# A recurrent attention and a cosine feed-forward on one core: eight chunks' bonus sums by TensorE, a fifth buffer for r, k and decays, first units in halves, a new plan of a block

## The chip, the cores and the metric

The kernel runs on one core of a Trainium2 chip. The metric is the device time of one execution in microseconds, the median of several runs; lower is better. Engines are named as in the profile: PE is TensorE (its weight loads apart as PEld), DVE is VectorE, ACT is ScalarE, POOL is GpSimd, SP is SyncE, which here only issues DMAs (SPq).

## The reference, cut to what matters

Two stages. The first is a linear recurrence with a decay per channel and a bonus `u` for the current step; the second is a feed-forward layer with `h * cos(h)` between two products.

```python
# r, k, v, w: (4 batches, 8 heads, 768 steps, 48)
for t in range(S):
    kt, vt, rt, wt = k[:, :, t], v[:, :, t], r[:, :, t], w[:, :, t]
    cur = einsum('bhd,bhe->bhde', u[None] * kt, vt)
    y[:, :, t] = einsum('bhd,bhde->bhe', rt, state + cur)
    state = wt[:, :, :, None] * state + einsum('bhd,bhe->bhde', kt, vt)
x = y as (3072 tokens, 384)
h = x @ w_in                 # (3072, 2048)
out = (h * cos(h)) @ w_out   # (3072, 384)
```

## The kernel before

**Chunks and blocks.** Time is cut into chunks of 128 steps; a chunk is one batch's 128 steps with all eight heads, as four pairs of heads. There are 24 chunks, in an order in which chunks 0 to 3 are the first of the four batches, 4 to 7 the second, and so on. Two chunks make a block (`BLK = 2`), so there are 12 blocks of 256 tokens: block 0 holds chunks 0 and 1, block 3 chunks 6 and 7.

**A chunk's steps**, by the letters that the plan uses:

- `load`: one DMA brings r, k and the decays, transposed, into a tile of the tag `tt` (`BUFS` gives four of them; 112 x 1541 numbers). `lv` loads v, `lr` loads r and k once more in natural layout (`rk`, in a buffer of the tag `h`, which the weights' words use too).
- `decay`: on DVE a scan backwards (`ee`, L208), its least value kept (L212), a reciprocal (L213), a scan forwards (L214); then r is multiplied by the forward products (`r3`, L218, DVE in the start and POOL later) and k by the backward ones (`k3`, L219).
- `diag`: the bonus sum r * u * k over a head's 48 channels, one number per step and head (`cd`). For chunks below `BY_PE` it is a product on DVE (`rkt`, L205) and a small matmul with u (`pc`, L225), copied out by ACT. For the others it is two products and a reduction on DVE from `rk` (L230, L231, L233). POOL then spreads `cd` over the diagonal of `asb` (L237).
- `a`: the scores, r against k (`pa`, L260), whose part above the diagonal DVE copies into `asb` (L262).
- `o` and `p`: what the chunk's own steps give (`py`, L315 and L320) and what the state gives (L330, L334), then the result as a high part (`xT`, ACT) and a low part (DVE, L144).
- `t` and `s`: k transposed (`pt`, L269, copied out as `kn`), then the chunk's addition to the state (`pst`, L287), and the new state `sn` (L292, L294). `d` (`dd`, L250) multiplies the state by the whole decay of the next chunk, on DVE in the start and on POOL later; ACT copies it to where `p` reads it.

**Units.** The 2048 columns between the products are 16 slices of 128; a block passes them two at a time, in 8 units. `mm1` is 18 matmuls into a bank of the kind `h` (`ph`, L382), 9 for each slice; then the gate: ACT (L358), DVE (L359), ACT (L360), DVE (L361), ACT (high part `gs`, L141), POOL (low part `gs`, L144, two instructions). `mm2` is 12 matmuls into two accumulators (`acc`, L400), of which the last four read the low part. Every product is three passes over high and low parts.

**Weights.** The 16 slices arrive as 64 bit numbers (`raw`) and are taken apart once, in the start (`w`): three instructions on ACT (L163, L166, L167) and a copy (L141), and three on DVE (L168, L169, and the low part L144) each. In the start the program's letters `f` and `w` fetch and take apart one slice.

**Order.** PE's order is written by hand throughout; DVE, ACT, POOL and SP are put in order by a scheduler, from the order in which the program is written and its own costs. `START` writes the first 16 units, which belong to blocks 0 and 1 in turns (`PAIR`), with chunks 0 to 7 between them. From block 2 on, `PLAN` has one row for each of a block's 8 units: `mm1`, an `mm2` that runs three units behind, and steps of chunks counted from the block's own, so `decay+4` in block 2 is that of chunk 8. A step that has not been done is done when another needs it (`NEEDS`).

**Banks.** In the start five banks serve attention; when block 0's first `mm2` comes it is three, while blocks 0 and 1 are both open two of each kind, and after block 1's last `mm2` three of each.

## Time and profile before

| | |
|---|---|
| time, median of 3 runs | 572.29 us (571.83 to 575.41) |
| the profiled execution's own time | 573.05 us |
| its span, first to last instruction | 571.2 us |
| mean granted TensorE clock over the span | 0.97 |
| PE busy, matmuls | 524.2 us, 92% of the span |
| DVE busy | 378.7 us, 66% |
| ACT busy | 270.1 us, 47% |
| POOL busy | 233.2 us, 41% |

The span is 1.85 us shorter than the time of the same execution. A busy PE is not a PE at its peak, and a share over the whole span hides stages of different kinds: up to about 66 us the weights are taken apart, up to about 145 us blocks 0 and 1 run side by side, and from there ten blocks run one after the other.

### The profile page before, as it was taken

Reading aid. Unit: us, or ns where it says so; the run is one execution under the profiler, and the core shown is the slowest. Engines: PE = TensorE matmul, PEld = TensorE weight load, DVE = VectorE, ACT = ScalarE, POOL = GpSimd, SP = SyncE. Lnnn points to the kernel's source line nnn. Section 1 sums busy time; section 2 is a strip of 40 time slices with the busy share of each in tenths; the row PEclk is TensorE's granted clock in tenths of the full one; section 3 lists DMA queues with packets and bytes.
Section 4 is the critical chain, followed back from the end, with each engine's and each line's share of the span. In section 5 each row is a group of like instructions: output and inputs, shape, how many; then the busy total and the mean of one; then the engine's idle time right before and its main releaser. Section 6 shows DMA issues by size and latency. Waiting matters only on the chain. (4 is left out here: it accounts for less than half of the span.)

```text
span 571.2 us, 11903 instructions
## 1 busy us (share of the span) xinstructions
PE 524.2 (92%) x4964; PEld 494.8 (87%) x4964; DVE 378.7 (66%) x560; ACT 270.1 (47%) x454; POOL 233.2 (41%) x286
## 2 busy tenths in 40 slices
PE   4658899985999999999999999999999999999996
PEld 3557889975899899899899899999899899999996
DVE  7989899985858558558548649548548447642331
ACT  2877997542342442452453353353352454444542
POOL 3033334463535434534534634534634532324332
PEclk9957899997999999999999999999999999999999
DMA  8955742116033034025025025025024017100000
GB/s 275 343 192 180 210 147 71 55 36 175 33 116 100 0 99 116 2 77 136 1 69 147 0 63 153 1 64 150 1 64 124 0 50 254 63 26 1 29 1 31
DMA packets 16728, 52.17 MB, mean 91 GB/s; under 512 B 2016, under 2 KB 8416, under 8 KB 16672
## 3 DMA queue, kind: packets, MB, share of 16 engines
q1 hardware_dynamic: 16528, 51.28, 29.6%
q8 instruction: 40, 0.66, 0.5%
q14 instruction: 16, 0.13, 0.1%
q10 hardware_dynamic: 144, 0.10, 0.1%
HBM read 46.65 MB, written 4.72 MB: 90 GB/s over the span
## 5 line engine op out<-in xcount | busy, mean ns | idle before, releaser
L144 POOL TENSOR_TENSOR gs<-rr,gs 128x256 fp32r<-128x256 f32 x192 | 157.9, 844 | 205.1 <-ACT gs L141 184.6
L382 PE MATMUL ph<-xT,w 128*128 128x256 f32 x1728 | 226.7, 286 | 15.4 <-ACT w L141 7.0
L382 PEld LDWEIGHTS ph<-xT,w 128*128 128x128 f32 x1728 | 216.7, 191 | 20.5 <-ACT w L141 7.5
L400 PE MATMUL acc<-w,gs 128*128 128x384 f32 x1152 | 226.1, 344 | 6.1 <-POOL gs L144 5.8
L400 PEld LDWEIGHTS acc<-w,gs 128*128 128x128 f32 x1152 | 199.0, 190 | 14.7 <-POOL gs L144 10.3
L360 ACT ACTIVATE rr<-rr,quarter 128x512 f32<-128x512 f32 x96 | 69.4, 723 | 159.7 <-DVE rr L359 159.7
L359 DVE SCALAR_TENSOR_TENSOR rr<-rr,ph 128x512 f32<-128x512 int32 x96 | 65.3, 680 | 70.6 <-ACT rr L358 58.8
L361 DVE TENSOR_TENSOR rr<-rr,ph 128x512 f32<-128x512 f32 x96 | 65.5, 682 | 44.6 <-ACT rr L360 44.3
L358 ACT ACTIVATE rr<-ph 128x512 int32<-128x512 f32 x96 | 57.0, 594 | 63.5 <-PE ph L382 63.4
L141 ACT CAST gs<-rr 128x512 fp32r<-128x512 f32 x96 | 58.8, 613 | 46.3 <-PE acc L400 43.3
L237 POOL TENSOR_SCALAR_AFFINE_SELECT asb<-cd 128x512 f32<-128x512 f32 x48 | 31.2, 674 | 53.2 <-PE py L320 28.0
L208 DVE TENSOR_TENSOR_SCAN ee<-tt,one_e 112x516 f32<-112x516 f32 x24 | 32.7, 1362 | 13.3 <-DMA tt<-tr 13.3
L218 POOL TENSOR_TENSOR tt<-tt 112x512 f32<-112x512 f32 x18 | 29.4, 1632 | 23.5 <-DVE tt L214 20.5
L262 DVE COPY_PREDICATED asb<-mask,pa 128x512 f32<-128x512 uint8 x48 | 32.7, 735 | 5.5 <-PE pa L260 4.2
L214 DVE TENSOR_TENSOR_SCAN tt<-tt,inj 112x516 f32<-112x516 f32 x24 | 34.8, 1452 | 0.1
L260 PE MATMUL pa<-tt 48*128 48x128 f32 x384 | 30.6, 304 | 3.2 <-DVE tt L219 2.2
L250 POOL TENSOR_TENSOR dd<-sn,ee 112x192 f32<-112x192 f32 x18 | 13.5, 753 | 48.9 <-DVE ee L208 48.9
L260 PEld LDWEIGHTS pa<-tt 48*128 48x128 f32 x384 | 25.7, 204 | 8.2 <-issue 4.3
L230 DVE TENSOR_TENSOR rk<-rk 128x384 f32<-128x384 f32 x18 | 15.7, 874 | 20.5 <-DMA rk<-tn 20.5
L287 PEld LDWEIGHTS pst<-v,kn 128*64 128x64 f32 (+1 forms) x320 | 11.4, 141 | 9.1 <-ACT kn L141 7.7
L287 PE MATMUL pst<-v,kn 128*64 128x48 f32 (+1 forms) x320 | 12.9, 233 | 6.9 <-ACT kn L141 6.9
L231 DVE TENSOR_TENSOR rk<-rk,u_sb 128x384 f32<-128x384 f32 x18 | 18.3, 1015 | 0.3
(67 smaller groups left out, 358.4 us busy)
## 6 DMA issues: line engine op xcount, KB each, us to landing
tt<-tr SPq DMA_DIRECT2D x22, 674.2 KB, 7.0
raw<-wts SPq DMA_DIRECT2D x16, 768.0 KB, 7.4
rk<-tn SPq DMA_DIRECT2D x18, 384.0 KB, 3.1
v<-tv SPq DMA_DIRECT2D x24, 224.0 KB, 6.7
ww<-w SPq DMA_DIRECT2D x6, 768.0 KB, 5.1
out<-ob SPq DMA_DIRECT2D x23, 192.0 KB, 2.0
tt<-tr SPq DMA_DIRECT2D x4, 224.0 KB, 4.5
tt<-tr SPq DMA_DIRECT2D x2, 226.2 KB, 3.7
```

What stands on the lines that cost most here:

```text
L141: (nc.scalar.copy if E[name] is nc.scalar else E[name].tensor_copy)(out=out, in_=in_)
L144: E[name].tensor_tensor(out=out, in0=full, in1=high.bitcast(F32), op=ALU.subtract)
L208: nc.vector.tensor_tensor_scan(out=ee.rearrange("p a t -> p (a t)")[:, ::-1], data0=wp[:, 1:W129 + 1][:, ::-1], data1=one_e.rearrange("p a ...
L214: nc.vector.tensor_tensor_scan(out=wp[:, 0:W129], data0=wp[:, 0:W129], data1=inj.rearrange("p a t -> p (a t)"), initial=0.0, op0=ALU.mult, ...
L260: nc.tensor.matmul(out=pa[h][:, p], lhsT=a["k3"][rows(h), p], rhs=a["r3"][rows(h), p], start=True, stop=True)
L262: nc.vector.copy_predicated(a["asb", h], mask, pa[h])
L358: nc.scalar.activation(nn, ph, AF.Copy, scale=INV2PI / W_SCALE, bias=0.25)
L359: nc.vector.scalar_tensor_tensor(out=rr, in0=nn, scalar=-2.0 * math.pi * W_SCALE, in1=ph, op0=ALU.mult, op1=ALU.add)
L360: nc.scalar.activation(rr, rr, AF.Sin, scale=1.0 / W_SCALE, bias=quarter)
L361: nc.vector.tensor_tensor(out=rr, in0=rr, in1=ph, op=ALU.mult)
L382: nc.tensor.matmul(out=ph[:, fi], lhsT=wgt[u * FU + fi][:, 0, a, kt * 128:(kt + 1) * 128], rhs=xT[:, b, kt], start=n == 0, stop=n == 3 * K ...
L400: nc.tensor.matmul(out=accs[i][j][:, :DM], lhsT=gs[:, a, fi, j * C:(j + 1) * C], rhs=wgt[u * FU + fi][:, 1, b], start=u == 0 and fi == 0 a ...
```

## The change

`BY_PE` goes from 6 to 8: chunks 6 and 7 get their bonus sums from `rkt` and `pc`, and no `rk` is loaded for them. `tt` gets a fifth buffer, `cd` and `rkt` a second one; `dd` has two instead of four. From block 2 on `dd` is made by DVE instead of POOL. `mm1` can be called for one slice of a unit; `START` calls it so (`m0`, `m1`), with the bonus sums and scores of chunks 2 and 3 between the halves of the first two units, and the own parts, transposes and state additions of chunks 0 to 3 earlier. `PLAN` has other places for `load`, `d` and `decay`.

```diff
-BY_PE = 6
+BY_PE = 8
...
-BUFS = dict(tt=4, v=4, h=2, rd=2, rr=7, gs=2, asb=4, sn=4, xT=2, kn=4, ee=2, dd=4, cd=1, rkt=1)
+BUFS = dict(tt=5, v=4, h=2, rd=2, rr=7, gs=2, asb=4, sn=4, xT=2, kn=4, ee=2, dd=2, cd=2, rkt=2)
...
-LATER = dict(... dd="p", ...)
+LATER = dict(... dd="v", ...)
...
-PLAN = ["t+2 t+3 mm1 mm2",
+PLAN = ["t+2 t+3 load+6 mm1 mm2",
...
-        "mm1 o+1 mm2 diag+5 p+1 lv+6 load+7 lr+7 load+6 x+2",
...
+        "mm1 o+1 mm2 diag+5 p+1 lv+6 lr+7 x+2",
+        "mm1 s+1 mm2 load+7 lv+7 x+3",
+        "mm1 mm2 d+4",
+        "mm1 mm2 decay+5",
+        "mm1 d+5 mm2 lr+6"]
-START = ["load0 load1 f lv0 decay0 f diag0 a0 lv1 decay1 diag1 a1 w load2 f w o0 mm1",
+START = ["load0 load1 f lv0 decay0 f diag0 a0 lv1 decay1 diag1 a1 w load2 f w o0 x0 decay2 diag2 m0 m1",
...
-    def mm1(t):
+    def mm1(t, part=None):
         i, u = seq[t]
-        weights("f", (u + 1) * FU + LEAD + FLEAD)
...
+        if not part:
+            weights("f", (u + 1) * FU + LEAD + FLEAD)
+            weights("w", (u + 1) * FU + LEAD)
+            for j in range(BLK):
+                att(i * BLK + j, "x")
+            units[t] = bank("h", [C, FU, BT], "ph")
+        xT, ph = xts[i], units[t]
+        for fi in range(FU) if part is None else (part,):
...
-        units[t] = gate(sb, ph)
+        if part is None or part == FU - 1:
+            units[t] = gate(sb, ph)
...
+                elif e in ("m0", "m1"):
+                    mm1(up1[0], int(e[1]))
+                    up1[0] += int(e[1])
```

What this does to the order is seen on the engines. First PE, after the own parts of chunks 0 and 1 (`py`), where the first units of block 0 begin; `w_181`, `w_195` are slices 0 and 1. Before:

```order
L382 MATMUL ph<-xT,w_181 128x256 x9
L382 MATMUL ph<-xT,w_195 128x256 x9
L382 MATMUL ph<-xT,w_278 128x256 x9
L382 MATMUL ph<-xT,w_297 128x256 x9
L225 MATMUL pc<-u_by_head,rkt 128x2 x4
L260 MATMUL pa<-tt 128x128 x8
```

After, up to the first `acc`:

```order
L225 MATMUL pc<-u_by_head,rkt 128x2 x4
L383 MATMUL ph<-xT,w_181 128x256 x9
L383 MATMUL ph<-xT,w_195 128x256 x9
L225 MATMUL pc<-u_by_head,rkt 128x2 x4
L383 MATMUL ph<-xT,w_298 128x256 x9
L260 MATMUL pa<-tt 128x128 x8
L383 MATMUL ph<-xT,w_330 128x256 x9
L260 MATMUL pa<-tt 128x128 x8
```

The bonus sums of chunks 2 and 3 moved ahead of and between the first units, and each chunk's scores stand behind one half of the second unit; before, chunk 3's `pc` and `pa` came only after the first `acc`.

Next DVE, in the last stretch in which blocks 0 and 1 run together, up to the low part of block 2's result (`xT`). Before:

```order
L230 TENSOR_TENSOR rk<-rk 128x384
L231 TENSOR_TENSOR rk<-rk,u_sb 128x384
L361 TENSOR_TENSOR rr<-rr,ph 128x512
L233 TENSOR_REDUCE cd<-rk 128x8 x2
L230 TENSOR_TENSOR rk<-rk 128x384
L231 TENSOR_TENSOR rk<-rk,u_sb 128x384
L230 TENSOR_TENSOR rk<-rk 128x384
L231 TENSOR_TENSOR rk<-rk,u_sb 128x384
L144 TENSOR_TENSOR xT<-py,xT 128x384 x2
```

After:

```order
L231 TENSOR_TENSOR rk<-rk,u_sb 128x384
L230 TENSOR_TENSOR rk<-rk 128x384
L231 TENSOR_TENSOR rk<-rk,u_sb 128x384
L359 SCALAR_TENSOR_TENSOR rr<-rr,ph 128x512
L262 COPY_PREDICATED asb<-mask,pa 128x512 x2
L361 TENSOR_TENSOR rr<-rr,ph 128x512
L359 SCALAR_TENSOR_TENSOR rr<-rr,ph 128x512
L361 TENSOR_TENSOR rr<-rr,ph 128x512
L359 SCALAR_TENSOR_TENSOR rr<-rr,ph 128x512
L361 TENSOR_TENSOR rr<-rr,ph 128x512
L144 TENSOR_TENSOR xT<-py,xT 128x384 x2
```

Of five `rk` products before `xT` two are left, and they stand ahead of four gates' instructions instead of directly before `xT`.

Last DVE in a block from block 2 on, from the low part of the next block's result. Before:

```order
L144 TENSOR_TENSOR xT<-py,xT 128x384 x2
L294 TENSOR_TENSOR sn<-pst,dd 112x192 x2
L233 TENSOR_REDUCE cd<-rk 128x8
L208 SCALAR_TENSOR_TENSOR ee<-tt,one_e 112x516
L359 SCALAR_TENSOR_TENSOR rr<-rr,ph 128x512
```

After:

```order
L144 TENSOR_TENSOR xT<-py,xT 128x384 x2
L294 TENSOR_TENSOR sn<-pst,dd 112x192 x2
L250 TENSOR_TENSOR dd<-sn,ee 112x192 x2
L208 SCALAR_TENSOR_TENSOR ee<-tt,one_e 112x516
L230 TENSOR_TENSOR rk<-rk 128x384
L212 TENSOR_SCALAR wholes<-ee 112x4
```

Two `dd` came in and one reduction went out ahead of the first scan; and a unit's L359 now stands behind `rk` and the scan's small steps.

## Rows read from the trace of the kernel before

**Rows 1.** Busy time in four stretches of the span: the stretch, its length, then PE, PEld, DVE, ACT and POOL busy us with their instructions, the granted clock (a share of 2.4 GHz), the DMA engines' share and GB/s.

```profile
0.00:66.00 66.00, 41.37 (x353) 36.82 (x354) 55.24 (x86) 46.77 (x63) 17.08 (x24) 0.82 0.70 238
66.00:107.00 41.00, 39.12 (x319) 37.97 (x318) 40.69 (x56) 35.19 (x55) 19.16 (x17) 0.99 0.41 121
107.00:145.00 38.00, 29.37 (x302) 27.27 (x301) 29.52 (x44) 11.05 (x22) 15.77 (x21) 0.87 0.34 92
145.00:572.00 427.00, 414.38 (x3996) 392.80 (x3995) 253.24 (x377) 177.10 (x315) 181.21 (x225) 1.00 0.23 66
```

**Rows 2.** The same view for one stretch in which the clock was low.

```profile
134.80:145.10 10.30, 6.73 (x57) 6.22 (x55) 5.92 (x11) 3.19 (x6) 1.93 (x3) 0.50 0.70 181
```

**Rows 3.** PE's waits: line, releaser, us in total, times, the longest.

```profile
PE acc L400 <- POOL gs L144: 5.8, 12, 0.7
```

**Rows 4.** DVE in order of time in the start: start, us, instruction, and in brackets the idle time before it and who ended it.

```profile
41.08 0.69 DVE L205 TENSOR_TENSOR rkt<-tt 112x512 f32<-112x512 f32 x1 [2.58 <-PE pc L225]
49.81 1.33 DVE L262 COPY_PREDICATED asb<-mask,pa 128x512 f32<-128x512 uint8 x2 [1.22 <-POOL asb L237]
64.51 0.62 DVE L292 COPY sn<-pst 112x192 f32<-112x192 f32 x2 [1.44 <-PE pst L287]
105.94 0.93 DVE L144 TENSOR_TENSOR w<-h,w 128x768 fp32r<-128x768 f32 x1
```

**Rows 5.** DVE in order of time from there to block 2's result, as above.

```profile
114.70 2.15 DVE L230 TENSOR_TENSOR rk<-rk 128x384 f32<-128x384 f32 x1
...
121.89 0.67 DVE L361 TENSOR_TENSOR rr<-rr,ph 128x512 f32<-128x512 f32 x1
...
133.26 1.01 DVE L144 TENSOR_TENSOR xT<-py,xT 128x384 fp32r<-128x384 f32 x2
```

**Rows 6.** ACT: the high part of block 2's result, and the copies of the transposed k of chunks 4 and 5.

```profile
126.19 0.86 ACT L141 CAST xT<-py 128x384 fp32r<-128x384 f32 x2
...
138.11 0.85 ACT L141 COPY kn<-pt 128x384 f32<-128x384 f32 x2
```

**Rows 7.** PE in order of time: the bonus sum of chunk 4, and then from the seventh unit of block 1 to the scores of chunk 7.

```profile
88.10 0.95 PE L225 MATMUL pc<-u_by_head,rkt 112*128 112x2 f32 x8
...
113.03 2.37 PE L382 MATMUL ph<-xT,w 128*128 128x256 f32 x18 [0.56 <-DVE rr L361]
...
118.25 2.39 PE L400 MATMUL acc<-w,gs 128*128 128x384 f32 x12
122.71 2.36 PE L382 MATMUL ph<-xT,w 128*128 128x256 f32 x18 [2.07 <-DVE rr L361]
124.91 2.28 PE L400 MATMUL acc<-w,gs 128*128 128x384 f32 x12
127.03 2.29 PE L382 MATMUL ph<-xT,w 128*128 128x256 f32 x18
129.15 2.28 PE L400 MATMUL acc<-w,gs 128*128 128x384 f32 x12
133.87 1.20 PE L269 MATMUL pt<-ident,tt 112*128 112x112 f32 x8 [2.43 <-DVE xT L144]
138.63 1.94 PE L287 MATMUL pst<-v,kn 128*64 128x48 f32 x32 [3.57 <-ACT kn L141]
140.50 1.83 PE L269 MATMUL pt<-ident,tt 112*128 112x112 f32 x8
...
156.50 1.16 PE L260 MATMUL pa<-tt 48*128 48x128 f32 x16 [1.03 <-ACT ob L413]
```

**Rows 8.** DVE behind that: the new states of chunks 4 and 5, and the second unit of block 2.

```profile
140.63 0.62 DVE L294 TENSOR_TENSOR sn<-pst,dd 112x192 f32<-112x192 f32 x2 [2.21 <-PE pst L287]
...
154.65 0.66 DVE L359 SCALAR_TENSOR_TENSOR rr<-rr,ph 128x512 f32<-128x512 int32 x1
```

**Rows 9.** One later block, PE, DVE and POOL in order of time.

```profile
272.94 0.62 PE L400 MATMUL acc<-w,gs 128*128 128x384 f32 x2 [0.65 <-POOL gs L144]
273.94 0.63 PE L400 MATMUL acc<-w,gs 128*128 128x384 f32 x2 [0.38 <-POOL gs L144]
...
258.24 0.54 DVE L233 TENSOR_REDUCE cd<-rk 128x8 f32<-128x384 f32 x1
260.45 1.23 DVE L208 TENSOR_TENSOR_SCAN ee<-tt,one_e 112x516 f32<-112x516 f32 x1 [1.67 <-DMA tt<-tr]
...
269.71 1.22 DVE L214 TENSOR_TENSOR_SCAN tt<-tt,inj 112x516 f32<-112x516 f32 x1
...
271.43 1.87 DVE L231 TENSOR_TENSOR rk<-rk,u_sb 128x384 f32<-128x384 f32 x1
...
268.00 1.03 POOL L250 TENSOR_TENSOR dd<-sn,ee 112x192 f32<-112x192 f32 x1
271.01 1.20 POOL L218 TENSOR_TENSOR tt<-tt 112x512 f32<-112x512 f32 x1 [1.98 <-DVE tt L214]
272.16 1.73 POOL L144 TENSOR_TENSOR gs<-rr,gs 128x256 fp32r<-128x256 f32 x2
```

**Rows 10.** Instructions by line and engine: count, shortest, median and longest ns, first and last start.

```profile
L294 DVE TENSOR_TENSOR sn<-pst,dd x16: 344/345/358, 140.6 to 430.1; 112x192 f32<-112x192 f32 x16
L250 POOL TENSOR_TENSOR dd<-sn,ee x18: 514/519/1142, 106.1 to 440.3; 112x192 f32<-112x192 f32 x18
L250 DVE TENSOR_TENSOR dd<-sn,ee x2: 773/835/897, 101.3 to 104.1; 112x192 f32<-112x192 f32 x2
```

More of the change, by code (lines that the diff above doesn't have):

```diff
@@ L48 @@
 EARLY = dict(rkt="v", cd="a", pc0="a", pc1="a", wadd="v", wm="a", whi0="a", whi1="a", ksh="a", gh="a", xh="a", rzh0="p", rzh1="v", r3="v", k3="v", rk="p", ru="p", rf0="v", rf1="v", kn="a", dd="v", rd0="a", rd1="a", rz0="v", rz1="v", ks="v", g0="p", g1="p", x="v", wlo0="v", wlo1="p", qf="s", qt="s", qr="s", qv="s", qx0="s", qx1="s", qo="s")
-LATER = dict(pc0="a", pc1="a", ksh="v", gh="a", xh="a", rzh0="a", rzh1="a", r3="p", k3="v", rk="v", ru="v", rf0="v", rf1="v", kn="v", dd="p", rz0="v", rz1="v", ks="p", g0="p", g1="p", x="v", qf="s", qt="s", qr="s", qv="s", qx0="s", qx1="a", qo="s")
+LATER = dict(pc0="a", pc1="a", ksh="v", gh="a", xh="a", rzh0="a", rzh1="a", r3="p", k3="v", rk="v", ru="v", rf0="v", rf1="v", kn="v", dd="v", rz0="v", rz1="v", ks="p", g0="p", g1="p", x="v", qf="s", qt="s", qr="s", qv="s", qx0="s", qx1="a", qo="s")
 OFF = 0
@@ L52 @@
 LEAD = 0
-PLAN = ["t+2 t+3 mm1 mm2",
+PLAN = ["t+2 t+3 load+6 mm1 mm2",
         "a+2 mm2 mm1 decay+4",
         "mm2 a+3 mm1 diag+4",
-        "mm1 o+1 mm2 diag+5 p+1 lv+6 load+7 lr+7 load+6 x+2",
-        "mm1 s+1 mm2 lv+7 x+3",
-        "mm1 mm2",
-        "mm1 mm2",
-        "mm1 d+4 d+5 mm2 decay+5 lr+6"]
-START = ["load0 load1 f lv0 decay0 f diag0 a0 lv1 decay1 diag1 a1 w load2 f w o0 mm1",
[4 rows of a table removed]
+        "mm1 o+1 mm2 diag+5 p+1 lv+6 lr+7 x+2",
[4 more added lines that the diff above has]
+START = ["load0 load1 f lv0 decay0 f diag0 a0 lv1 decay1 diag1 a1 w load2 f w o0 x0 decay2 diag2 m0 m1",
[4 rows of a table added]
 PAIR = "0001110101010101"
@@ L368, in gate @@
         return gs
-    def mm1(t):
+    def mm1(t, part=None):
         i, u = seq[t]
-        weights("f", (u + 1) * FU + LEAD + FLEAD)
-        weights("w", (u + 1) * FU + LEAD)
-        for j in range(BLK):
-            att(i * BLK + j, "x")
-        xT = xts[i]
-        ph = bank("h", [C, FU, BT], "ph")
-        for fi in range(FU):
+        if not part:
[6 more added lines that the diff above has]
+        for fi in range(FU) if part is None else (part,):
             n = 0
@@ L522, in rwkv_cos_ffn @@
             for e in row.split():
-                if e in ("mm1", "mm2"):
-                    up(int(e[-1]) - 1)
+                if e == "mm2":
+                    up(1)
+                elif e in ("m0", "m1"):
+                    mm1(up1[0], int(e[1]))
+                    up1[0] += int(e[1])
                 elif e in ("f", "w"):
```

8 rows, old and new, of the table START are left out of this document.

## The prediction, made before the changed kernel ran

> **What bounds the kernel now.** I read the stages first, then PE's waits, then each engine in order of time where PE waits.
>
> The stages [rows 1]: up to 66 us PE is busy 41 of 66 us at a mean clock of 0.82, and DVE 55: the start follows the engines that take the weights apart and prepare chunks. From 66 to 107 us DVE is busy 40.7 of 41.0 us and PE 39.1, at full clock: both near their bound. From 107 to 145 us PE falls to 29.4 of 38 us. From 145 us on PE is busy 414 of 427 us and DVE 253: PE bounds ten blocks, and what other engines do counts only where a matmul waits for it.
>
> PE's waits say where that is. In the later blocks it is one place: the last four matmuls of an `mm2` wait for POOL's low part of `gs`, 5.8 us in 12 waits [rows 3], in the seven blocks (2 to 8) in which the next decays are made. Between 113 and 157 us PE loses more: 0.56, 2.07, 2.43, 3.57 and 1.03 us in waits [rows 7], and a low clock, 0.50 of 2.4 GHz (the 1.2 GHz level), from 134.8 to 145.1 us [rows 2], which began right behind two waits 3.6 us apart. The reason is DVE's order: it takes five `rk` products, the first at 114.70 us, before block 2's `xT`; ACT's half of `xT` was ready at 127.05 us [rows 6], DVE began the other at 133.26 us [rows 5], PE's transposes waited for that until 133.87 us, and `kn`, behind two gates on ACT, came at 138.11 us.
>
> So the path is DVE up to about 122 us, the hand-over of block 1 to block 2 until about 157 us, then PE with one wait in seven blocks.
>
> **The start, up to the last weight.** DVE as a clock: the low part of the last slice ends at 106.87 us [rows 4]. Counting DVE's instructions up to it in both orders, after has one `rkt` more (0.69), one scan more (1.23, [rows 9]) and one L359 less (0.66, [rows 8]): +1.2 us. Three waits of DVE [rows 4] lose their cause: 2.58 us for the only `rkt` buffer, which PE freed late; 1.22 us for POOL's diagonal, which stood behind a unit's low part and now is ahead of it; 1.44 us for `pst`, since DVE has other work there now. Together 5.2 us. Against that, a new wait: `pst` of block 0 stands ahead of the third unit, and `kn` on ACT behind the weights' instructions, so by my estimate from both orders PE waits some 5 us at about 50 us and DVE, by the order, up to 1 us for the gate behind it. Bounds: all 5.2 saved, or 1 of them. I take 4.2 - 1.2 = 3: the last slice ends at 104 us.
>
> **The hand-over.** From 106.87 us to the end of the L361 that frees a bank for the eighth unit, 122.56 us [rows 5], DVE took 21 instructions in 15.7 us. The change needs 19 of these kinds until the L361 that frees the bank for block 1's seventh unit: without one L361 (0.6 from start to start), one scan (1.2) and one reduction (0.5), with one `rkt` (0.7): 14.1 us, so 118.1 us, where it was 113.03 us. PE starves a few us before. But now nothing more of `rk` stands ahead of the gates and `xT`, transposes come before the last unit, and a unit and an `mm2` cover `kn`. PE's work from there to the end of `pst`, by the starts of [rows 7]: the unit, own and state parts 5.2 us (113.03 to 118.25), three `mm2` and two units of 2.12 us each (124.91 to 127.03 to 129.15), transposes and `pst` about 2.0 (1.20 and 1.94 us there, the second at the low clock), in all 17.8 us: it ends at 135.9 us, before at 140.50 us. Lead: 4.6 us.
>
> Behind `pst` DVE decides: from the new states to block 2's second L359 it took 14.0 us (140.63 to 154.65, [rows 8]), and on ACT the eviction that frees a bank for chunk 7's scores stands behind that gate; the scores waited 1.03 us. After, two `dd` (0.35 to 0.90 each, [rows 10]) come in and 1.4 us of small waits go. So PE waits some 3 us at that place, the lead stays at 4.6 to 5, and the two added bonus sums on PE (0.95 each, [rows 7]) lie in that wait. The starving at 107 to 118 us may drop the clock as the two waits at 133.87 and 138.63 us did; matmuls then take twice as long for some us, up to 4 us lost, which I price at 1. **Start and hand-over: 4 us gained, bounds 0 and 8.**
>
> **The blocks.** PE's wait follows POOL: the low part began at 272.16 us, directly behind `r3` (271.01 us), which waited for DVE's second forward scan (269.71 us) [rows 9]. So the term is how far that scan moves against the state's end at 258.24 us, 12.7 us before it. Gone: a reduction (0.54) and the wait for the first decays (1.67), since the fifth buffer lets that load go a block earlier. Added: two `dd` and an L231 that stood behind the scan. L231 takes 0.56 us, or 1.87 beside POOL [rows 9]. `dd` on DVE is not seen here but in the start, at 0.77 and 0.90 us beside POOL's work; an instruction of the same shape takes 0.35 [rows 10]. POOL has nothing to do in that place after the change, so I take 0.50: 2 x 0.50 + 0.56 - 2.21 = -0.65 us. The ends are -0.95 and 2 x 0.90 + 1.87 - 2.21 = +1.46 us. POOL's own `dd` cost nothing here: one ended two us before `r3` could begin. At -0.65 us the first half of the wait goes, and the second (0.38) mostly stays: 0.6 us in each of seven blocks. **Blocks: 4 us gained; bounds 6 gained (all of [rows 3]) and 10 lost (7 x 1.46).** The load of `rk` stays directly ahead of `xT`, as before; nothing on PE waits for that `xT` for 18 us. SP's queue: the late load of the second decays keeps its place behind PE's state part, the early one waits for nothing.
>
> The second `cd`, the two `dd` instead of four and `check_decays` cost nothing by this: each `dd` has been read by ACT and by `sn` a block before its buffer is needed.
>
> **Sum.** 573.05 - 8 = 565.05 us for an execution like the profiled one; the median of the runs stood 0.76 us lower, so 564.3 us. A measurement of this kernel tells about 1%, 5.7 us, from no change.
>
> **The rivals.**
>
> *DVE's `dd` stays slow (chance 0.27).* If it takes what its two rows took, 0.84 us, the scan moves by 2 x 0.84 + 0.56 - 2.21 = 0.03 us, the blocks gain nothing, and 4 us from the start remain: 568.3 us. For it: no row of a fast one. Against it: POOL should be idle there. The same time comes if the hand-over gives nothing and the blocks do. The Trainium skill, on the page "SBUF — State Buffer" ("Who interferes with whom"), has a rule on this side: a DVE instruction with two SBUF inputs contends with a GpSimd instruction that reads SBUF, and who comes later is blocked. `dd` has two such inputs on either engine, so by that rule the move does not take it out of POOL's way. The trace agrees: POOL's own took 1.03 us at 268.00 us against a median of 0.52.
>
> *More of both (0.15).* The clock holds, the wait for the eviction is short: the start gives 8 us, the blocks all 6: 558.3 us. For it speaks that DVE is ahead in every stretch; against it, that the hand-over has a wait at each step that I could find.
>
> *Slower: the blocks' scan comes late (0.08).* DVE now does `dd`, `rk` and L231 before the second forward scan. If it needs more than the 12.7 us from the state's end, POOL's `r3` and the low part are late by the difference, in seven blocks. At the upper ends, +1.46 us, that is 10 us; with 4 us from the start 578.3 us. For it: L231's 1.87 us beside POOL. Against it: POOL has less to do there than before.
>
> *Nothing (0.05).* The earlier loads and second buffers lie where nobody waits, and DVE's order eats the rest: 572.3 us.
>
> **How the numbers follow.** The forecast has 0.45, with 560 to 569 us of its own. Of it three quarters lie beyond 1%: 0.34; with "more of both" 0.15 and a fifth of the first rival 0.05 that gives 0.54 for faster. Within 1%: 0.11 + 0.22 + 0.05 = 0.38. Slower 0.08. The range reaches from "more of both" to a blocks' term that loses a little: 558 to 574 us.
>
> **What the changed kernel's profile would show.** DVE without the 2.58 us wait for `rkt`; the last slice's low part at about 104 us; `pst` of block 2 ending at about 136 us and no low clock from 135 to 145 us; chunk 7's scores waiting about 3 us for ACT's eviction; in blocks 2 to 8 the first forward scan's tile without a wait for its DMA, `dd` at about 0.5 us on DVE, and PE's wait for POOL's low part under 3 us in total. The prediction is wrong if PE's early wait for `kn` (some 5 us at 50 us) is not hidden by DVE's lateness behind it, if the clock stays low through the hand-over, or if the blocks find a new wait.

## The result, and the profile after

The changed kernel took 551.28 us, median of four runs (550.59 to 554.87), against 573.55 for the kernel before (571.83 to 575.41) beside it: a ratio of 0.9627 with a 95% interval of 0.9579 to 0.9675, 21 us. The forecast was 564.3 us, range 558 to 574: the sign holds, the gain is between two and three times the one I summed, and the time lies below the range. The profiled execution took 554.87 us (span 553.1), the slowest of the four, against 573.05 (span 571.2); so the two traces below are 18 us apart, not 21.

The stages of the changed kernel, as in [rows 1]:

```profile
0.00:66.00 66.00, 42.33 (x361) 37.92 (x362) 59.88 (x94) 48.41 (x65) 14.71 (x22) 0.79 0.81 266
66.00:107.00 41.00, 40.00 (x327) 38.73 (x326) 40.16 (x59) 32.67 (x52) 25.18 (x21) 1.00 0.35 102
107.00:145.00 38.00, 34.55 (x359) 32.39 (x358) 24.85 (x39) 15.86 (x31) 14.35 (x18) 0.96 0.22 60
145.00:553.00 408.00, 401.01 (x3939) 382.83 (x3938) 239.27 (x385) 173.54 (x310) 161.42 (x209) 1.00 0.23 67
```

PE is busy 5.2 us more from 107 to 145 us, in the hand-over from block 1 to block 2. Behind that PE bounds as before, but the stretch is 19 us shorter. In part that is the lead that PE has at 145 us (57 matmuls less are left, 3939 against 3996); the rest are waits and the pace of its steps, below. PE's waits over the whole span, the longest and the one for POOL:

```profile
PE pc L225 <- DVE rkt L205: 13.4, 4, 7.4
...
PE acc L402 <- DVE asb L262: 2.8, 1, 2.8
...
PE acc L402 <- POOL gs L144: 0.2, 1, 0.2
```

The waits for POOL's low part [rows 3] are down to 0.2 us. In the start PE now waits 13.4 us for `rkt` in four waits, where the kernel before had one of 7.5 us.

The hand-over, answering to [rows 4, 7, 8]: first DVE's low part of the last weight slice, then PE, then DVE's new states of chunks 4 and 5 and its second L359 of block 2.

```profile
99.93 0.94 DVE L144 TENSOR_TENSOR w<-h,w 128x768 fp32r<-128x768 f32 x1
```

```profile
115.11 3.32 PE L383 MATMUL ph<-xT,w 128*128 128x256 f32 x18 [1.92 <-DVE rr L361]
...
133.29 1.13 PE L287 MATMUL pst<-v,kn 128*64 128x48 f32 x32
134.35 0.60 PE L269 MATMUL pt<-ident,tt 112*128 112x112 f32 x4
...
147.61 1.16 PE L260 MATMUL pa<-tt 48*128 48x128 f32 x16
```

```profile
134.47 0.62 DVE L294 TENSOR_TENSOR sn<-pst,dd 112x192 f32<-112x192 f32 x2 [0.37 <-PE pst L287]
...
145.54 0.66 DVE L359 SCALAR_TENSOR_TENSOR rr<-rr,ph 128x512 f32<-128x512 int32 x1
```

The state part ends at 134.35 us (140.50 before), and chunk 7's scores begin at 147.61 without a wait (156.50 before): the lead is 6.2 and then 8.9 us.

A later block, answering to [rows 9], PE, DVE and POOL:

```profile
257.56 2.26 PE L383 MATMUL ph<-xT,w 128*128 128x256 f32 x18
259.66 2.25 PE L402 MATMUL acc<-w,gs 128*128 128x384 f32 x12
261.74 0.93 PE L269 MATMUL pt<-ident,tt 112*128 112x112 f32 x8
...
247.34 0.62 DVE L250 TENSOR_TENSOR dd<-sn,ee 112x192 f32<-112x192 f32 x2
247.88 1.22 DVE L208 TENSOR_TENSOR_SCAN ee<-tt,one_e 112x516 f32<-112x516 f32 x1
...
255.02 1.46 DVE L231 TENSOR_TENSOR rk<-rk,u_sb 128x384 f32<-128x384 f32 x1
...
257.00 1.22 DVE L214 TENSOR_TENSOR_SCAN tt<-tt,inj 112x516 f32<-112x516 f32 x1
...
252.17 2.22 POOL L144 TENSOR_TENSOR gs<-rr,gs 128x256 fp32r<-128x256 f32 x2 [7.22 <-DMA tt<-tr]
254.34 1.72 POOL L218 TENSOR_TENSOR tt<-tt 112x512 f32<-112x512 f32 x1
258.30 1.20 POOL L218 TENSOR_TENSOR tt<-tt 112x512 f32<-112x512 f32 x1 [2.24 <-DVE tt L214]
259.45 2.89 POOL L144 TENSOR_TENSOR gs<-rr,gs 128x256 fp32r<-128x256 f32 x4
```

The first scan has no wait for its load, both `dd` together take 0.62 us while POOL is idle, and the `mm2` at 259.66 us goes through in 2.08 us from start to start.

One thing more is in these rows and was in no sum: a step of PE, 18 matmuls of `ph` or 12 of `acc` without a wait, takes 2.10 and 2.09 us until the next one begins (medians of all such steps behind 160 us). In the kernel before it was 2.13 and 2.12, down to the last blocks, at the same granted clock of 1.00 (2.4 GHz). Here are three steps of the kernel before, in PE's order of time:

```profile
513.18 2.29 PE L382 MATMUL ph<-xT,w 128*128 128x256 f32 x18
515.30 2.28 PE L400 MATMUL acc<-w,gs 128*128 128x384 f32 x12
517.42 2.29 PE L382 MATMUL ph<-xT,w 128*128 128x256 f32 x18
```

### The profile page after: what moved, and what is told of

The parts are those of the page before. It is cut to its first block, busy times and chain, and to the rows that moved or that the text cites. A ratio compares the mean times of both kernels' runs of the same rounds, so it can differ in the third digit from the quotient of the medians.

```text
span 553.1 us, 11951 instructions
## 1 busy us (share of the span) xinstructions
PE 517.9 (94%) x4980; PEld 491.9 (89%) x4980; DVE 364.2 (66%) x574; ACT 270.5 (49%) x456; POOL 215.7 (39%) x268
## 5 line engine op out<-in xcount | busy, mean ns | idle before, releaser
L402 PE MATMUL acc<-w,gs 128*128 128x384 f32 x1152 | 222.1, 342 | 5.0 <-DVE asb L262 2.8
L359 DVE SCALAR_TENSOR_TENSOR rr<-rr,ph 128x512 f32<-128x512 int32 x96 | 65.6, 683 | 81.2 <-ACT rr L358 67.7
L361 DVE TENSOR_TENSOR rr<-rr,ph 128x512 f32<-128x512 f32 x96 | 65.3, 680 | 47.2 <-ACT rr L360 47.2
L237 POOL TENSOR_SCALAR_AFFINE_SELECT asb<-cd 128x512 f32<-128x512 f32 x48 | 34.3, 747 | 43.0 <-PE py L320 23.3
L218 POOL TENSOR_TENSOR tt<-tt 112x512 f32<-112x512 f32 x18 | 23.6, 1309 | 28.3 <-DVE tt L214 27.1
L214 DVE TENSOR_TENSOR_SCAN tt<-tt,inj 112x516 f32<-112x516 f32 x24 | 32.4, 1349 | 0.1
L141 ACT COPY past<-dd 48x192 f32<-48x192 f32 x40 | 14.0, 351 | 25.0 <-DVE dd L250 24.5
L225 PE MATMUL pc<-u_by_head,rkt 112*128 112x2 f32 x64 | 10.4, 285 | 13.4 <-DVE rkt L205 13.4
L225 PEld LDWEIGHTS pc<-u_by_head,rkt 112*128 112x128 f32 x64 | 10.3, 243 | 14.2 <-DVE rkt L205 7.9
L230 DVE TENSOR_TENSOR rk<-rk 128x384 f32<-128x384 f32 x16 | 10.9, 678 | 15.5 <-DMA rk<-tn 15.5
L219 DVE TENSOR_TENSOR tt<-tt,ee 112x512 f32<-112x512 f32 x24 | 19.8, 824 | 0.0
```

Of the source, the lines that this page charges most:

```text
L141: (nc.scalar.copy if E[name] is nc.scalar else E[name].tensor_copy)(out=out, in_=in_)
L214: nc.vector.tensor_tensor_scan(out=wp[:, 0:W129], data0=wp[:, 0:W129], data1=inj.rearrange("p a t -> p (a t)"), initial=0.0, op0=ALU.mult, ...
L237: nc.gpsimd.affine_select(out=asb, in_=col.unsqueeze(2).to_broadcast([C, NP, C]), pattern=[[0, 4], [1, C]], compare_op=ALU.is_equal, fill= ...
L359: nc.vector.scalar_tensor_tensor(out=rr, in0=nn, scalar=-2.0 * math.pi * W_SCALE, in1=ph, op0=ALU.mult, op1=ALU.add)
L361: nc.vector.tensor_tensor(out=rr, in0=rr, in1=ph, op=ALU.mult)
L402: nc.tensor.matmul(out=accs[i][j][:, :DM], lhsT=gs[:, a, fi, j * C:(j + 1) * C], rhs=wgt[u * FU + fi][:, 1, b], start=u == 0 and fi == 0 a ...
```

## The experiments

All runs by kernel. The ratio is to the kernel before, timed beside it on the same chip. The last two columns are from each trace: A is the start of block 3's past part (L334), up to which the start and the hand-over lie, B the time from there to the first matmul of `pv`, with which the check of the decays ends behind the last units; in B lie the blocks in which PE bounds. A row with "and" adds to the row above it. Kernels with "b" or "l" start from the kernel before, the others from the changed one.

A and B are of one execution each. The kernel before gave 166.8 and 165.6 us, 393.1 and 395.5 us, so a difference of 2 us or so between two rows tells nothing by itself. Where a time is taken from two ratios, the interval behind it is that of both together.

| kernel | what differs | us | ratio (95%) | A | B |
|---|---|---|---|---|---|
| before | | 573.55 | 1 | 166.8 | 393.1 |
| c0_before | nothing | 573.5 | | 165.6 | 395.5 |
| b_pad | tiles 64 bytes up | 570.73 | 0.9970 (0.9948 to 0.9991) | 166.2 | 390.8 |
| b_tt5 | fifth buffer | 566.14 | 0.9881 (0.9849 to 0.9913) | 166.5 | 385.2 |
| l_dd | and dd on DVE | 558.59 | 0.9716 (0.9679 to 0.9752) | 160.8 | 385.4 |
| l_later | and new plan | 559.46 | 0.9741 (0.9672 to 0.9810) | 160.8 | 385.2 |
| o_six | and second rkt, cd | 553.67 | 0.9670 (0.9640 to 0.9701) | 159.3 | 381.5 |
| a_oldstart | and eight chunks | 551.57 | 0.9605 (0.9567 to 0.9644) | 157.5 | 382.3 |
| after | and first order | 551.28 | 0.9627 (0.9579 to 0.9675) | 157.9 | 383.1 |
| a_pad | after, tiles 64 up | 555.68 | 0.9697 (0.9673 to 0.9721) | 156.6 | 385.7 |
| a_ddpool | after, dd on POOL | 559.35 | 0.9755 (0.9686 to 0.9823) | 157.8 | 387.6 |
| s_start | and old plan | 558.99 | 0.9725 (0.9654 to 0.9796) | 158.9 | 387.7 |
| p_tail | a_ddpool, check one place later | 557.94 | 0.9736 (0.9704 to 0.9768) | 159.7 | 387.0 |
| p_nocheck | a_ddpool, no check | 553.10 | 0.9638 (0.9577 to 0.9700) | 158.6 | 383.5 |
| a_nocheck | after, no check | 552.89 | 0.9644 (0.9587 to 0.9701) | 156.0 | 382.4 |
| o_oldplan | a_oldstart, old plan | 548.77 | 0.9596 (0.9568 to 0.9624) | 153.4 | 382.1 |
| o_ddpool | o_oldplan, dd on POOL | 557.82 | 0.9714 (0.9665 to 0.9762) | 156.5 | 388.0 |
| o_pad128 | o_oldplan, tiles 128 up | 554.04 | 0.9664 (0.9623 to 0.9706) | 155.1 | 386.9 |
| o_best | a_oldstart, writes by ACT | 550.58 | 0.9608 (0.9577 to 0.9640) | 157.4 | 381.6 |
| o_best2 | o_oldplan, writes by ACT | 547.67 | 0.9547 (0.9505 to 0.9589) | 155.4 | 381.7 |

### The pace of a step: c0_before, b_pad, a_pad, o_pad128

`c0_before` is the kernel before, with no edit.

> The kernel before, unchanged, profiled once more on the chip of the runs below. In the two profiles at hand a step of 18 or 12 matmuls that waits for nothing begins 2.12 us after the last one before the change and 2.095 us after it, at a granted clock of 1.00 in both, down to the last blocks where nothing but TensorE's own order is left; over some 190 such steps that is 4 to 5 us of the 18 us between the two spans. If the chip or the moment of the profile makes that, this profile shows 2.095 us here too. If it belongs to the program (where its tiles lie, or what stands in TensorE's queue), this one shows 2.12 us again.

Measured: 2.125 and 2.12 us again (medians behind 160 us). It is not the chip or the moment; the program has this pace.

`b_pad` and `a_pad` (and later `o_pad128`) make `cd` wider at both of its places, to 24, 16 and 24 columns; the order of instructions stays the same on every engine:

```diff
-            cd = buf("cd", [C, 8], F32)
+            cd = buf("cd", [C, 24], F32)[:, :8]
```

> The kernel before with one tile made wider: cd takes 96 bytes of a partition instead of 32, so that what lies behind it, xT and gs among them, moves up by 64 bytes (xT from 174688 to 174752). Every engine's instructions and their order are the same. In the traces so far the step of TensorE follows the place of xT and gs: 2.125 us for 18 matmuls of ph and 2.12 for 12 of acc where xT begins 96 bytes past a multiple of 128 (before), 2.10 and 2.09 at 32 past (the changed kernel), 2.145 and 2.085 at 0 past (the later part alone). My theory, that the place alone does this: steps of 2.10 and 2.09 us here and 4 to 5 us less, 568 to 569. Rival, that it comes from what else is queued: 2.125 and 2.12 again, 573.

> The changed kernel with each of the two cd at 64 bytes instead of 32, which moves xT and gs up by 64 bytes, to 96 past a multiple of 128, as they lay before the change; the order of all instructions is the same. My theory: steps of 2.125 and 2.12 us come back, 4 to 5 us more, 555 to 556. Rival, that the place counts for nothing: 551.

> The run with old first order and old plan, with each of the two cd at 96 bytes instead of 32, so that xT and gs begin 32 bytes past a multiple of 256 instead of 160; the order of all instructions is the same. The paces seen so far, ph and acc in us per step, by the place of xT past a multiple of 256: 96: 2.125 and 2.12; 128: 2.145 and 2.085; 160: 2.10 and 2.09; 224: 2.155 and 2.10. My theory, that the place modulo 256 (not 128) counts: a pace of its own, somewhere from 2.09 to 2.16, and a time that differs from 548.8 by the pace times 96 steps of each kind, so 548 to 555. Rival, that it is the place modulo 128 after all: 2.10 and 2.09 again, 548.8.

Measured, one `acc` step of each, from its start to that of the `ph` step and from there to the next, in PE's order of time. `b_pad` (160 bytes past a multiple of 256):

```profile
512.98 2.25 PE L400 MATMUL acc<-w,gs 128*128 128x384 f32 x12
515.07 2.26 PE L382 MATMUL ph<-xT,w 128*128 128x256 f32 x18
517.17 1.03 PE L400 MATMUL acc<-w,gs 128*128 128x384 f32 x5
```

`a_pad` (224):

```profile
501.88 2.26 PE L402 MATMUL acc<-w,gs 128*128 128x384 f32 x12
503.97 2.32 PE L383 MATMUL ph<-xT,w 128*128 128x256 f32 x18
506.13 2.08 PE L402 MATMUL acc<-w,gs 128*128 128x384 f32 x11
```

`o_pad128` (32):

```profile
501.40 2.28 PE L402 MATMUL acc<-w,gs 128*128 128x384 f32 x12
503.52 2.30 PE L383 MATMUL ph<-xT,w 128*128 128x256 f32 x18
505.66 1.58 PE L402 MATMUL acc<-w,gs 128*128 128x384 f32 x8
```

So `b_pad`, with the kernel before's instructions, has the changed kernel's pace, 2.10 and 2.09 us, and the place of the tiles alone does it. I had expected the old pace from `a_pad`; it got another one, 2.155 and 2.10. With `o_pad128` at 2.14 and 2.12 (32 past, as 160 is modulo 128) the place modulo 128 doesn't decide. Of the 4 to 5 us that I expected, `b_pad` kept 1.7 (0.5 to 3.0); its waits for POOL stayed at 5.8 us. Where PE has few other waits the place counts more: 4.0 ± 3.1 us by the ratios of `a_pad` and the changed kernel (0.9697 and 0.9627), 3.9 ± 2.9 by those of `o_pad128` and `o_oldplan` (0.9664 and 0.9596).

### The fifth buffer: b_tt5

```diff
-BUFS = dict(tt=4, v=4, h=2, ...
+BUFS = dict(tt=5, v=4, h=2, ...
```

> The kernel before with five buffers of tt instead of four and nothing else. The start-alone run had the old plan and dd on POOL and yet no waits for POOL's low part (0.7 us), and its blocks took 41.6 us against 43.3 before. My theory: the fifth buffer does it, since the first scan of a chunk no longer waits for its load (13.3 us of such waits before, all later blocks together) and hands r3 to POOL earlier; blocks of 41.8 to 42.0 us here (xT lies as in the later-part run, ph at 2.145), 1.5 us less in each of 7 or 8 blocks, so 560 to 563. Rival, that the loads must also be issued at other places of the plan: waits for POOL as before and 571 to 574.

Measured: 566.1, B from 393.1 to 385.2, no wait for POOL's low part left, blocks of 41.8 us. The blocks are as expected, but the gain is 6.8 ± 1.8 us and not the 10 to 13 that I gave, and the reason I gave does not hold: DVE's first scan still waits for its load, and the second forward scan begins 14.9 us behind the start of the state part, as before (15.0). What has changed is POOL's order. In `b_tt5`, POOL in one later block and the `mm2` of the same place:

```profile
261.73 2.12 POOL L218 TENSOR_TENSOR tt<-tt 112x512 f32<-112x512 f32 x1
264.78 3.00 POOL L144 TENSOR_TENSOR gs<-rr,gs 128x256 fp32r<-128x256 f32 x2 [0.93 <-ACT gs L141]
267.75 1.19 POOL L218 TENSOR_TENSOR tt<-tt 112x512 f32<-112x512 f32 x1
```

```profile
256.25 1.23 DVE L208 TENSOR_TENSOR_SCAN ee<-tt,one_e 112x516 f32<-112x516 f32 x1 [1.56 <-DMA tt<-tr]
```

```profile
266.66 2.25 PE L400 MATMUL acc<-w,gs 128*128 128x384 f32 x12
268.74 0.93 PE L269 MATMUL pt<-ident,tt 112*128 112x112 f32 x8
```

The gate's low part now stands ahead of the second `r3` (L218), where it stood behind it [rows 9]. PE's step takes 2.08 us. In the kernel before, the step of [rows 9] with its two waits took 3.69 us from start to start, though the waits shown add up to 1.03:

```profile
270.71 1.58 PE L400 MATMUL acc<-w,gs 128*128 128x384 f32 x8
...
274.40 0.93 PE L269 MATMUL pt<-ident,tt 112*128 112x112 f32 x8
```

### dd's engine: a_ddpool, s_start, l_dd, o_ddpool

In the changed kernel (`a_ddpool`), and in `o_oldplan` (`o_ddpool`):

```diff
-LATER = dict(... kn="v", dd="v", ...
+LATER = dict(... kn="v", dd="p", ...
```

`s_start` takes the old `PLAN` besides; `l_dd` is `b_tt5` with `dd="v"` and `dd=2`.

> The changed kernel with dd back on POOL in the later blocks and nothing else. My theory: POOL again has dd ahead of the gate's low part in some blocks, and TensorE waits 3 to 6 us for it, so 554 to 558. Rival, that the moved loads and the fifth buffer removed the waits (the scan at the new place comes early enough) and dd's engine does not count: 551 to 552.

> The changed kernel with the plan of a later block and dd's engine as before: what is left of the change is the first order in halves, eight chunks by TensorE, the second rkt and cd, the fifth buffer of tt. My theory, with the sizes that the changed kernel's trace shows: the start and the hand-over give about 9 us (first scores of block 3 at 147.6 us against 156.5), and the later blocks keep their 5 to 6 us of waits for POOL's low part, so 8 to 10 us under the kernel before, 562 to 565. Rival, that the whole change is one thing (the start moves the later blocks into a better place): 552 to 555. Rival, that the start alone gives what the prediction said: 568 to 570.

> The kernel before with five buffers of tt, and dd on VectorE with two buffers; plan, first order and six chunks as before. Block 3's past part stood at 166.5 us with the fifth buffer alone and at 160.8 us when the new plan and dd on VectorE came with it; behind it both took 385.2 us to the vote. My theory, from the run with the old plan, which lost nothing: dd's engine makes that lead; past part at 160 to 162 us and 558 to 561 in time. Rival, that the plan makes it: 166 us and 565 to 567.

> The run with old first order and old plan (548.8; block 3's past part at 153.4 us, 382.1 us from there to the vote) with dd back on POOL and nothing else; left of the change are eight chunks by TensorE, two rkt and cd and the fifth buffer. My theory: the reductions of the check stand ahead of the last chunk's masked copy again (4 to 5 us), and the hand-over loses what dd's engine gave there, so 553 to 559. Rival, that with the bonus sums gone from VectorE dd's engine counts only for the check: 552 to 554.

Measured: dd's engine is worth 9.5 ± 2.8 us (`b_tt5` to `l_dd`), 7.3 ± 4.8 (`a_ddpool` to after) and 6.8 ± 3.2 (`o_ddpool` to `o_oldplan`), and in none of them through POOL's low part: with dd on POOL PE waits for it 0.7 us in `a_ddpool` and `s_start` and not at all in `b_tt5` and `o_ddpool`, where I had expected 3 to 6 of `a_ddpool`. `a_ddpool` came out 1 us above what I gave it, `s_start` 3 us below. The traces show the gain in two places, one for each set of other parts.

The hand-over, with six chunks: A falls by 5.7 us from `b_tt5` to `l_dd`, and `l_later` has the same 160.8. With eight chunks A tells less. In the new order it is 157.8 to 159.7 us in the four kernels with dd on POOL and 156.0 to 157.9 in the three with dd on DVE. From `o_ddpool` to `o_oldplan` it falls by 3.1 us, but `o_pad128`, with the order of `o_oldplan`, and `o_best2`, which differs from it up to there in little more than who issues the writes, have 155.1 and 155.4. The mean granted clock from 100 us to A goes with it: 0.94 in `o_ddpool`, 0.97 in these two, 1.00 in `o_oldplan`. DVE in `b_tt5`, and in `l_dd`:

```profile
115.51 2.21 DVE L208 TENSOR_TENSOR_SCAN ee<-tt,one_e 112x516 f32<-112x516 f32 x1
...
121.04 0.65 DVE L361 TENSOR_TENSOR rr<-rr,ph 128x512 f32<-128x512 f32 x1
```

```profile
117.13 0.69 DVE L361 TENSOR_TENSOR rr<-rr,ph 128x512 f32<-128x512 f32 x1 [0.32 <-ACT rr L360]
...
137.37 1.22 DVE L208 TENSOR_TENSOR_SCAN ee<-tt,one_e 112x516 f32<-112x516 f32 x1
```

In `b_tt5` a ninth chunk's backward scan (and its forward scan at 119.90 us) stands ahead of block 2's `xT`, directly before gates that free PE's bank. In `l_dd` eight chunks are scanned up to there, and the ninth comes behind the new states (135.16 us), at 137.37 us; `xT` begins at 127.78 us instead of 133.62. The instructions are the same but for dd's engine: only their order on DVE differs.

The last blocks, with eight chunks: B is 387.0 to 388.0 us in the four kernels with the check and dd on POOL, 381.6 to 383.1 in the five with dd on DVE and the same place of xT. With six chunks it is the same on either engine (385.2 and 385.4). `a_ddpool` on PE and on DVE:

```profile
450.24 0.43 PE L315 MATMUL py<-asb,v 128*32 128x128 f32 x8 [3.06 <-DVE asb L262]
```

```profile
447.80 1.75 DVE L351 TENSOR_REDUCE top<-ww 128x1 f32<-128x1536 f32 x1 [2.31 <-DMA ww<-w]
449.46 1.34 DVE L262 COPY_PREDICATED asb<-mask,pa 128x512 f32<-128x512 uint8 x2
```

The check's reduction, which waits for its load, stands ahead of the last chunk's masked copy, and PE waits 3.06 us for that. In the changed kernel the copy is ahead:

```profile
445.07 1.37 DVE L262 COPY_PREDICATED asb<-mask,pa 128x512 f32<-128x512 uint8 x2
447.47 1.75 DVE L351 TENSOR_REDUCE top<-ww 128x1 f32<-128x1536 f32 x1 [1.03 <-DMA ww<-w]
```

The kernel before has no such wait either. So with eight chunks dd on DVE does not win these 4 to 5 us over the kernel before; it avoids a loss that the other parts would have brought.

### Is it the check's place? p_tail, p_nocheck, a_nocheck

```diff
-            if t >= slots - NU + 2 and n_checked[0] < WCH:
+            if t >= slots - NU + 3 and n_checked[0] < WCH:
```

in `p_tail`; `n_checked[0] < 0` in the other two, which so leave the check of the decays' size out.

> The run with dd on POOL, with the check of the decays put one place later in the last blocks; nothing else. In that run's trace VectorE has a reduction of the check, which waits 2.31 us for its load, ahead of the last chunk's masked copy, and TensorE waits 3.06 us for that copy at 450 us; in the changed kernel the copy stands ahead of the reduction. My theory: half of what dd on POOL cost (559.35 against 551.3) is that place, so 555 to 556 here. Rival, that it is dd's own time on POOL in every block: 559.

> The run with dd on POOL without the check of the decays' size at the end: the six loads of w and their reductions on VectorE are left out (the vote then goes by the least decay product alone). To be compared with the changed kernel without the same check. My theory: what dd's engine cost was mostly the reduction ahead of the last chunk's masked copy (TensorE's wait of 2.7 to 3.1 us at 450 us and the low clock behind it in two of three traces), so the two kernels without the check differ by 1 to 2 us only. Rival, that dd on POOL costs its 6 to 8 us in every block: they differ by 6 to 8.

> The changed kernel without the same check, for comparison with the run before. In the changed kernel no wait of TensorE ends on a reduction of the check. Both theories: 550 to 552, as with the check.

Measured: `p_tail` told nothing. The reductions came one unit later in the code, but on DVE the fifth still stands ahead of the copy (447.55 and 449.21 us), and PE waits 2.67 us. Without the check dd's engine counts for nothing by the times (553.10 and 552.89, each with an interval of some 3.5 us either way), and B is 383.5 and 382.4. The place is seen more sharply in the stretch from one past part (L334) to the next that holds it: 44.4 us in `a_ddpool`, 45.6 to 45.8 in `s_start`, `p_tail` and `o_ddpool`, where the granted clock fell behind the wait (0.66 from 450 to 455 us in the first two of these), against 40.7 in the changed kernel and 40.6 in `p_nocheck`. So in the last blocks the cost of dd on POOL was the place that the reductions then took, not dd's own time.

### What the rest is worth: l_later, o_six, a_oldstart, o_oldplan

`l_later` is `l_dd` with the new `PLAN`; `o_six` adds `cd=2, rkt=2`; `a_oldstart` adds `BY_PE = 8`, which is the changed kernel with the old `START`; `o_oldplan` is that with the old `PLAN`.

> The kernel before with the later part alone: new plan of a block, dd on VectorE with two buffers, five buffers of tt; first order, six chunks by TensorE as before. My theory: the start stays as it was (last weight slice at about 107 us, first scores of block 3 at about 156 us), the waits of TensorE for POOL's low part fall from 5.8 us to under 1, so 6 us under the kernel before, 566 to 568; with the shorter step of 2.095 us, if that belongs to this part, 5 us more, 561 to 563. Rival, that dd's place is worth nothing without the early start: 571 to 574.

> The changed kernel with the first order of before (whole units, chunks 2 and 3 after the second and third unit); eight chunks by TensorE, two rkt and cd, fifth buffer, new plan, dd on VectorE stay. The later part alone gave 559.5 with a pace of ph that costs about 2 us more than the changed kernel's. My theory: the first order is worth 4 to 6 us (last weight slice at 106 us again instead of 100), so 555 to 557. Rival, that the bonus sums and the buffers give the lead and the order gives nothing: 551 to 552.

> The changed kernel with the first order of before, as in the old-first-order run, and six chunks by TensorE instead of eight; so it differs from the later-part run by the second rkt and cd (and where xT lies) alone, and from the old-first-order run by the bonus sums of chunks 6 and 7 alone. My theory: the bonus sums are worth the lead that the old-first-order run has at 107 us (22.4 steps begun against 21.0), 1.4 steps of 2.1 us, and what chunks 6 and 7 cost DVE at 108 to 125 us; so 3 to 5 us more than its 551.6, 555 to 557. Rival, that the second rkt and cd made the lead and the six or eight chunks count for nothing: 551 to 552.

> The old-first-order run with the old plan of a block too; what is left of the change is eight chunks by TensorE, the two rkt and cd, the fifth buffer of tt and dd on VectorE. The plan moves one load, one decay and one dd by up to four places. My theory: with five buffers the loads are early at either place, and the plan is worth nothing: 551 to 553. Rival, that the plan with dd on VectorE makes the 7 us between the fifth buffer alone (566.1) and the later part (559.5): 557 to 559.

Measured: `l_later` took 559.5 us, under the 566 to 568 that I gave it, and it does not have the shorter step of the 561 to 563; I had no term for the hand-over, where A fell by 6 us. The new first order gives nothing that the runs can tell (`a_oldstart` 551.57, changed kernel 551.28; -1.3 ± 3.5 us by the ratios), though its last weight slice is done at 100.9 us against 104.3. It changes one wait for another; PE's waits up to 62 us in `a_oldstart`:

```profile
PE pc L225 <- DVE rkt L205: 7.4, 1, 7.4
PE ph L383 <- ACT w L141: 6.6, 2, 3.4
PE ph L383 <- DVE w L144: 3.5, 3, 1.5
```

and in the changed kernel, beside the 13.4 us for `rkt` and 2.8 for `asb` above:

```profile
PE ph L383 <- DVE w L144: 2.4, 2, 1.7
...
PE ph L383 <- ACT w L141: 0.5, 1, 0.5
```

At 107 us the old order has begun 22.4 steps of `ph` and `acc`, the new one 21.8, the kernel before 20.5. So the rival held there. The new plan gives nothing that the runs can tell either (-1.4 ± 4.5 us from `l_dd` to `l_later`, -0.5 ± 2.7 from `o_oldplan` to `a_oldstart`), and with eight chunks and the old first order it may cost something: A is 157.4 and 157.5 us in the two kernels with it, 153.4 to 155.4 in the three without. The second `rkt` and `cd` give 4.1 ± 4.3 us by the ratios of `l_later` and `o_six`; in the traces it is 3.7 us of B, most of which is the place of xT, as `ph` goes from 2.145 to 2.10 us a step. Eight chunks give 3.7 ± 2.8 us (`o_six` to `a_oldstart`), inside the 3 to 5 I gave; in medians it is 2.1, but the two ran on different chips. It is not by the lead at 107 us that I named: `o_six` has that too (22.9 steps). By 135 us it has begun 29.0 steps, `a_oldstart` 31.0, so the gain comes between. That it is made by the bonus sums of chunks 6 and 7, which are off DVE there, is likely but was not shown apart.

### A faster version: o_best, o_best2

The output's writes are issued by ACT: `qo="a"` in `LATER`.

> The old-first-order run with the output's writes issued by ScalarE, which makes the output, instead of SyncE. In its trace the loads of r and k for chunks 8 and 9 stand behind four writes of the first two blocks' output on SyncE's queue, which end 142 to 148 us; VectorE waits 3.60 us for that load at 162 us with scans behind it, and TensorE 1.26 us for the gate at 175 us, in a block that takes 44.1 us where the next take 41.4. My theory: with the writes off that queue the wait goes and this block takes 41.4 to 42 us, so 2 to 3 us less than 551.6, 548.5 to 550. Rival, that issuing writes costs ScalarE as much in later blocks: 551 to 553.

> The run with old first order and old plan, with the output's writes issued by ScalarE. There the block behind the start still takes 43.2 us against 41.4 of the next, with TensorE waiting 0.7 us for the gate behind VectorE's late load of r and k. My theory: that block goes to 41.4 to 42.6, 1 to 2 us less than 548.8, 547 to 548. Rival, that it gives nothing, as moving the writes gave 1 us at the most in the run with the new plan: 548.5 to 549.5.

Measured: the block behind the start goes from 44.1 to 42.6 us in `o_best` and from 43.2 to 42.5 in `o_best2`, and DVE's wait for the load of `rk` there from 3.60 to 0.73 us and from 2.88 to 1.09. In time that is nothing in the first pair (-0.2 ± 2.9 us by the ratios) and 2.8 ± 2.9 in the second, both inside what the runs tell. `o_best2`, which has the fifth buffer, dd on DVE, eight chunks and the second `rkt` and `cd`, but neither the new first order nor the new plan, has the lowest time here: 547.67 us, ratio 0.9547 (0.9505 to 0.9589), under the changed kernel by 3.6 us in medians and by 4.6 ± 3.7 in ratios.

## Why the prediction was right in sign and wrong in size

Four steps of the sum failed: DVE taken as the clock of the start, the 3 us wait for the eviction in the hand-over, the price of PE's waits for POOL (5.8 us of idle time, where 9.8 us were lost), and the pace of a step, which had no term.

By the ratios in the table, each times 573 us, the way from before to after is: fifth buffer 6.8 us, dd's engine 9.5, plan -1.4, second `rkt` and `cd` with the place of xT 4.1, eight chunks 3.7, first order -1.3, in all 21.4; each has the interval given above; by the ratios alone the plan, the first order and, just, the second `rkt` and `cd` can't be told from nothing. By the traces it is 8.9 us in A, where I had 4 to 5, and 10.0 in B, where I had 4. The clock has little part in that: up to A the mean granted clock was 0.90 in both kernels, and over the rest 1.00 but for the last microseconds.

**The start** was wrong as a step. I took DVE's time for the clock of the start, and its lead at the end of the last slice (3 us forecast, 6.0 measured, 106.87 to 100.87 us) for a lead of the path. The signs came: DVE's 2.58 us wait for `rkt` is gone. But PE has longer waits for `rkt` (5.72 us at 31 us) and a new one for `asb` (2.85 us at 47 us) instead, and `a_oldstart` reaches block 3 at the same time without the new order. PE's wait of some 5 us for `kn` at about 50 us, which I had counted against it, did not come. The lead of A is there without the new order: with dd on DVE, the second `rkt` and `cd`, and eight chunks A falls from 166.5 to 157.5 us, though each of the last two steps (1.5 and 1.8 us) is within what A varies by.

**The hand-over** was right up to the state part: the unit behind L361 began at 115.1 us (118.1 forecast), `pst` ended at 134.35 (135.9), and the clock was not low from 135 to 145 us. It fell instead from 116.2 to 119.6 us (0.51, the 1.2 GHz level), behind PE's waits of 1.12 and 1.92 us; by the starts of the unit at 115.11 us and the parts behind it that cost some 1.6 us, my estimate from the rows of both kernels, where I had priced 1. One reading of mine was wrong: the low clock of [rows 2] began at 134.8 us, behind the wait that ended at 133.87 us, but ahead of the one that ended at 138.63, and not behind both. Wrong as a step was the eviction: chunk 7's scores should have waited 3 us for it and did not wait. I had carried the 14.0 us of [rows 8] over, less 1.4 us of waits, and put two `dd` on top. From the new states (134.47 us) to block 2's second L359 (145.54) it was 11.1 us: waits of 0.30, 0.26 and 1.10 us are gone, L212 took 0.14 us where it had taken 1.69 at 149.85 us, and the two `dd` took 0.38 and 0.33. So the lead grew to 8.9 us instead of staying at 4.6 to 5.

**The blocks** were right in what they saw in the changed kernel, a second forward scan that comes earlier and a PE that no longer waits for POOL, but the reason was only one of two, and the size was wrong three times. The fifth buffer does not work as I said: alone it leaves the wait for the first decays and the scan where they were, and yet the waits for POOL went, by POOL's order. That the forecast had the end of these waits right is in part luck. Of the sizes, first comes the price of a wait: I took the idle time of [rows 3], 5.8 us, as all there was. From start to start the seven steps took 3.82, 3.83, 3.69, 3.68, 2.97, 3.41 and 3.21 us where 2.12 is normal: 9.8 us. In these seven steps a wait cost more than the idle time shown. Second, how far the scan moves: 0.65 us forecast, but it began 13.2 us behind the start of the state part, against 15.0 before, and `dd` took 0.32 to 0.38 us, not 0.50 (most of the rest is that the first forward and the second backward scan took 1.21 and 1.20 us where [rows 9]'s block had 1.78 and 1.69); PE's wait went to 0.2 us, as the sign "under 3 us" had it. Third, the pace of a step had no term at all; 0.055 us for each pair of steps would be some 4 us over B's 78 pairs, an estimate of which `b_pad`, in the kernel before, kept 1.7. Against these stands the block behind the start, 44.0 us where others take 41.4: DVE waits there 3.49 us for a load of `rk` and PE later 1.27 us for the gate. That the output's writes ahead of it in the queue do this fits `o_best`, but `a_pad`, with the writes where they were, had a block of 42.4 us too.

**dd's engine** I priced by its own duration alone ("POOL's own `dd` cost nothing here"). True for POOL, and yet 7 to 9.5 us hang on it, because the order of DVE's other instructions came out differently. No duration of the kernel before shows that; the orders of the kernels with and without each part do.

**The rivals.** That `dd` stays slow (0.27) is refuted: 0.32 to 0.38 us in all twenty. POOL ran nothing beside 17 of these, as in the block above, where it was idle from 244.95 to 252.17 us. So the Trainium skill's rule on two SBUF inputs ("SBUF — State Buffer", "Who interferes with whom"), that such an instruction on DVE contends with one of GpSimd that reads SBUF, is not against it. L231, which has two such inputs too, took 0.52 to 0.56 us in the twelve places where POOL ran nothing, and 1.02 to 2.88 us in the four where it did (1.46 us at 255.02 us beside POOL's `r3`), so the trace agrees with the rule. "Slower" (0.08) is refuted too, since the second forward scan came earlier, and "nothing" (0.05) by the time. "More of both" (0.15; 558.3 us) is nearest, and its bounds, 8 for the start and 6 for the blocks, were too narrow for the reasons above.
